# Loading q and k of tiles 2 to 5 of the first batch by token pairs, with VectorE and TensorE putting them in order, in a fused attention and MLP kernel with a hand-written order

## The chip, the cores and the metric

The kernel runs on one core of a Trainium2 chip. The metric is the device time of one execution in microseconds, the median of several runs. The clock that TensorE was granted stands at 1.000 in the profile shown.

## The reference, cut to what matters

Local attention with a few global keys, for 4 batches of 8 heads, 768 tokens and head dimension 64; its output, seen as 3072 tokens by 512, goes through an MLP of width 2048 with a squared ReLU.

```
scores = q @ k.T / sqrt(D)                      # (4, 8, 768, 768)
keep   = (key < 8) | (0 <= query - key < 96)    # 8 global keys, 96 local ones
scores = where(keep, scores - slope[h] * dist, -1e9)
attn   = softmax(scores) @ v                    # (4, 8, 768, 64)
x      = attn.transpose(0, 2, 1, 3).reshape(3072, 512)
out    = relu(x @ w_in) ** 2 @ w_out            # w_in 512x2048, w_out 2048x512
```

Since a query sees the keys of its own and of the preceding tile of 128 tokens, and the global ones, the kernel computes two 128x128 blocks of scores for each tile and head, "own" and "before".

## The kernel before

**Tiling.** A batch of 768 tokens is two halves of 384, and a half is three tiles of 128 tokens; the halves are H0 to H7. For each half come, in this order: loads of q, k and v from HBM with a cast from fp32 to fp16 (`list_loads`, `rows`, L491, issued by GpSimd, the engine POOL in the profile); q and k turned so that the head dimension lies on the partitions; scores (TensorE), exponentials (ScalarE, ACT in the profile), a product with a mask (VectorE, DVE), the product with v (`av`), a division (`norm`), the turn of the result into `xt`; then layer 1 (`hps`) and layer 2 (`yps`) of the MLP with fp16 weights, in part by a scheme that saves products by adding and subtracting blocks first (`in_mix`, `x_mix`, `mixed`, `w_mix`).

**The first batch, H0 and H1.** It is worked tile by tile, in the order that the list `OPENING` names: `T0`, `T1` turn tiles 0 and 1 (their q and k come by four HWDGE loads of token pairs in fp32, L539, which VectorE casts, L355), `Q2` to `Q5` and `K2` to `K5` turn the q and k of one tile (`turn_tile`, L1368: four 128x128 transposes into one PSUM bank, then one copy of 128x512), `P` puts the distance biases into PSUM (L1390), `S` adds the scores (L1411), `A` is the product with v (L1461), `X` turns its result (L1490), `F`, `G`, `D` and `E` are layer 1. q and k of tiles 2 to 5 come by eight loads of one tile each: 128 partitions, 8 heads, rows of 64 fp32 elements, 256 bytes each. Those of tile 2 land in `sk` and `sq`; those of tiles 3 to 5 land in the memory of `w_mix`, which nothing else uses so early. `LOADING` gives the order in which the loads of the first batch are numbered, with the four parts of `w_in` (c0 to c3) among them.

**The later halves.** H2 is turned by TensorE (`turn`, L650), H3 to H7 by DMA transposes on SP's queue (`turn_by_dma`, L670). `sk` and `sq` are single buffers: the loads of a half wait until the half before it has been turned. The results of attention go into `xt` by DMA transposes, too (`to_x_by_dma`, L801). The rows of the global keys of H3 are copied into `vb` by a DMA (`fix_globals`, L625).

**What sets the order.** Each step is an `Op` with its needs. The string `ORDER` lists all steps: `p` for TensorE's, by number, with the PSUM banks behind the point, `l` for the loads, and `a`, `d` and `s` for those of ACT, DVE and SP. `by_table` emits them in that order, so each engine's queue is fixed, in order, and an instruction that waits holds up everything behind it. A number behind `@` makes a load wait for a DMA transpose (six loads before, four in the changed kernel). The loads of POOL take turns on eight semaphores, so a load is issued only when the one eight places ahead of it has landed.

Of the kernel before, what the change touches and what calls it, by code (L numbers as in the profile page):

```python
# [10 lines left out]
FP16 = mybir.dt.float16  # L11
# [3 lines left out]
P = 128  # L15
# [5 lines left out]
OPENING = """T0 P1b T1 K3 P0o S0o S1b Q2 K2 P1o S1o P2o P2b A00 S2o A01 S2b Q5 Q3 A11 X01 Q4 V1 S3o A10  # L21
K4 X11 A20 X00 K5 X10 A21 S4o S4b S3b X21 X20 F1 G11 V2 S5o V3 S5b G10 F0 A40 V4 A30 G01 A41
# [4 lines left out]
LOADING = """v1 k3 k2 q2 v0 q3 q4 q5 k5 v2 k4 c1 v3 c0 v4 v5 c3 c2"""  # L27
# [26 lines left out]
ORDER = """d1 s8 g2 a4 p0.0 a6 s10 d12 a0 d13 l1 l2 l3 d146 a26 d15 d20 d3 a22 l0 a30 d9 d21 a18 d5 a17 a16  # L54
l4 d14 a19 p1.12 a27 p5.34 a28 d11 l5 a29 p10.56 d7 a23 l7 p3 l8 p4.7 l9 l6 a32 a31 a24 d37 p6 d33
a34 p2.07 a39 d35 p8.1 d36 p7 a40 d43 p11 l10 a25 a41 p9.2 p13.31 a46 d44 p12.40 l11 a42 d45 p14.2
d59 p17 a47 l12 p15 d48 a52 p16.5 p24.7 p19.6 d51 p20.2 a49 l13 d55 a53 p21.3 p18.5 d64 l14 a50
p28.4 p23.61 d56 a69 p27.7 d54 l16 p31.0 a57 d38 p26.4 p34.23 a60 d72 l17 p29.5 d68 p22.6 a61
p35.0 d70 l15 l18 a81 d58 p25.1 p30.7 a85 p36.2 d65 a82 p39.50 l23 d86 a71 d66 p32.63 a92 p33.12
d67 d63 l19 p40.74 a77 d91 p38.5 a78 d83 d62 d80 p37.1 a73 d79 d84 a74 p44.2 l22 p41.6 a93 d107  # L60
a87 d76 l21 p47.3 l20 a97 p52.2 p45.0 a89 d111 l27 d96 a119 p48.1 a98 d75 l28 a101 p46.3 l29 p43.7
d110 p53.5 p42.2 d105 l30 d95 p50.4 p55.6 a103 l25 p49.3 d116 d94 a120 a112 p59.7 l24 a102 d88
d106 a90 p51.4 a108 d189 p60.2 a114 d100 a104 d99 p56.5 a113 d191 a122 p57.1 p65.0 d125 p54.3 d138
a117 p63.6 p62.4 a128 d121 a109 p58.7 d139 d129 d130 p61.1 a118 p67.0 d115 a132 d272 d133 a131
p70.3 a135 p71.2 a126 d142 p72.1 p69.6 a162 d127 p82.4 d190 a156 d192 a165 p66.7 a159 l31 a157
a160 p64.0 d205 d158 l26 d163 a123 d161 p84.6 d134 a140 d206 l36 d143 d166 p83.3 d207 a136 l35
d164 p81.2 a167 d187 a141 p85 l33 d124 a137 d186 p79.57 a184 l34 l32 d147 p88.10 p80.34 a178 p77.2
a195 p74.5 a181 d201 d202 a196 d204 p68.1 d203 a179 d151 a182 p73.3 d208 d180 a144 p90.0 d183 a145
p86 a174 a168 d152 a169 p75.7 d154 p78.41 d153 p89.23 p87 a175 d148 a198 p100.5 a176 d155 a193
d150 p98.4 s194 l38 p91.2 a185 d197 l39 a199 d228 p76.1 a209 d177 a210 l37 p96.6 s229 a171 p105.3  # L70
p107 p92 d200 a172 d225 a173 p93.4 s216 p94 d170 a188 d149 p95.7 a211 a240 d236 s217 p97 d214 d219
d237 p104 d212 s220 p102.1 a245 p103.6 s226 d213 d238 a244 d227 d223 d221 p101 d218 p106 l45 a222
s224 p99 l41 d246 a241 s242 d239 s215 p109.47 d234 p108.06 p111 a251 a248 p118.2 d243 a252 d258
p110.14 l43 s235 s247 a249 d273 p116.07 l40 p113 d230 a255 l42 d250 l44@224 a256 d254 p112 a268
d253 d231 p119.6 d257 a269 p114.14 l47 d270 p115.07 p124 a261 d274 l46 p120 a283 d259 a264 s275
p122.1 a262 p129.6 d280 p121.5 s325 a265 d232 p127.0 d267 p126 d276 a287 p133.4 d285 p134.7 d295
a286 s324 p117.3 d263 a290 p123.4 a278 p140 d266 a271 p130 d281 a307 p128.5 p135 a291 a308 d233
p132 d298 p136 d294 a279 p131.3 d300 s282 a299 p137.1 l48@324 a297 p138 a303 d323 d301 p139 p125.4
a302 p142 d288 d304 a292 p143.7 d305 a310 d311 p141.1 d326 l49 s296 a284 a312 p144.6 a309 d293
s289 l52 a306 p145.53 d313 p146.02 p147.47 a327 d318 p148.1 a333 d433 d319 a322 l54 p149.5 a330  # L80
d336 a328 d314 l53 p151.41 d320 a331 p150.03 p152 a337 d329 l51 a338 d332 p157.2 a339 p153 d321
a341 d316 a344 a350 l50 a334 p172.0 l65 d315 a342 d345 p159.3 d340 p158.4 p161 d335 a355 p164.5
a352 p155.7 d370 p154.1 s277 p163 a347 d351 s371 p168.0 d395 p162 p169.4 d317 d358 a364 p156 a348
s398 p174.0 d356 a366 d343 a365 p171.7 d359 s399 l56 p177 p160.3 d369 a378 p165 l55 a360 p167 d357
s346 d353 a363 p173.5 p166.7 a372 p178.2 a362 s260 d373 p175 d349 a361 p180 d375 p182.3 s374 p179
d382 a379 p176 p170 d380 p183 d385 p181.0 a381 s354 p184 a376 a383 s386 p185.2 d367 d400 a387
p186.53 d384 a389 p188.71 a388 l60@371 p187.04 d368 d377 a413 l59 p189.6 a406 d401 d405 l57 a414
d402 p190.7 a409 d404 l62 d403 a407 p191 a410 l63 p193.51 a417 d416 a418 p194.03 d415 p192.46
l61@386 p195 d476 d411 a419 s390 d391 a426 l64 d408 l58 p196 p206.4 d393 a422 p198.0 d397 a420
p197.5 a434 d396 l74 a423 p219.6 d392 a432 d412 a427 d394 p210 d429 p218.1 a445 d477 a462 d424  # L90
p208 d480 a461 p204.7 d431 a448 p205.3 d421 p215.4 a444 p203.6 d443 p214 d442 a458 s491 l66 p199.1
# [209 lines left out]
def kernel(  # L301
# [1268 lines left out]
    jobs = {}  # L1570
# [115 lines left out]
```

## Time and profile before

| | us |
|---|---|
| three runs: median (lowest to highest) | 204.44 (203.87 to 205.93) |
| the profiled execution's own time | 204.62 |
| its span, first to last instruction | 202.8 |
| TensorE busy | 192.3 (95% of the span) |
| DVE busy | 177.4 (87%) |
| ACT busy | 146.5 (72%) |
| POOL busy | 66.7 (33%), nearly all of it issuing loads |

The profiled execution took 0.18 us more than the median of the runs; 1.8 us of its time lie outside its span. In the rows of the profile, PE is TensorE's matmul, PEld its weight load, and SPq and ACTq are the DMA issues of SP and ACT. A row of the timeline gives the start, the time until its last instruction ended, the engine, the line, what is written from what, and how many instructions were merged; in brackets stands the idle time ahead of it and what ended it.

### The profile page before, as it was taken

The page shows a single profiled execution, that of the slowest core. Times are in us where ns is not written, and L with a number is a line of the kernel's source. Part 1 is how long each engine was busy: PE and PEld are TensorE (multiplying, and loading weights), DVE is VectorE, ACT ScalarE, POOL GpSimd, SP SyncE. Part 2 cuts the span into 40 slices and gives each one's busy share as a digit, 9 for nine tenths or more (in the row PEclk, how much of TensorE's full clock was granted, in tenths as well). Part 3 has the DMA queues.
Part 4 walks back from the last instruction along what each step waited for, and adds up shares of the span by engine and source line. Part 5 has one row for each costly group of instructions (what it writes and reads, how often), then busy time and mean ns, then how long its engine had stood idle before and what let it go on. Part 6 is the DMA issues. An engine that isn't in the chain of part 4 may idle for free.

```text
span 202.8 us, 5878 instructions
## 1 busy us (share of the span) xinstructions
PE 192.3 (95%) x2348; PEld 161.7 (80%) x2348; DVE 177.4 (87%) x448; ACT 146.5 (72%) x310; POOL 66.7 (33%) x82
## 2 busy tenths in 40 slices
PE   7798999999999899999895999999999999999994
PEld 3676999866798587789783898889888899898993
DVE  6799789999995799999893999899999999989781
ACT  5799877988826679978783877977888676475221
POOL 8995637538006700790261702910000000000000
PEclk9999999999999999999999999999999999999999
DMA  5999999999999999999999993999632330020214
GB/s 158 177 148 193 198 178 176 206 187 157 167 182 114 192 132 166 91 177 131 221 128 140 96 180 81 164 165 147 179 109 73 95 80 15 0 107 0 103 55 155
DMA packets 106987, 27.52 MB, mean 136 GB/s; under 512 B 97104, under 2 KB 104016, under 8 KB 106960
## 3 DMA queue, kind: packets, MB, share of 16 engines
q0 software_dynamic: 74944, 13.11, 90.2%
q1 hardware_dynamic: 30816, 13.45, 31.6%
q10 hardware_dynamic: 1200, 0.59, 1.1%
q8 instruction: 18, 0.29, 0.7%
q14 instruction: 9, 0.07, 0.1%
HBM read 27.26 MB, written 6.29 MB: 165 GB/s over the span
## 4 chain that ended last, share of the span: by engine, by line
PE 44%; DMA 40%; POOL 8%; SPq 3%; issue 2%; DVE 2%; ACT 1%; POOLq 0%; DVEq 0%
PE yps L1145 22%; PE hps L925 14%; DMA sq<-in_q_dram 10%; DMA sk<-in_k_dram 7%; DMA w_out_sb<-in_moe_w_out_dram 6%; DMA xt<-tm 5%; PE hps L822 5%; DMA k<-sk 5%; DMA w_in_sb<-in_moe_w_in_dram 4%; POOL w_mix L491 3%; SPq L670 3%; DMA q<-sq 3%; POOL sk L491 2%; PE av L776 2%; POOL sq L491 2%
## 5 line engine op out<-in xcount | busy, mean ns | idle before, releaser
L822 PE MATMUL hps<-xt,w_in_sb 128*128 128x384 f16 (+2 forms) x336 | 45.4, 280 | 2.5 <-DMA xt<-tm 2.1
L728 ACT ACTIVATE ex<-sp 128x512 f16<-128x512 f32 x66 | 35.2, 619 | 7.1 <-PE sp L715 6.5
L1145 PEld LDWEIGHTS <-h 128*128 128x128 f16 x376 | 34.1, 98 | 4.5
L822 PEld LDWEIGHTS <-w_in_sb 128*128 128x128 f16 x336 | 28.1, 98 | 9.0 <-issue 0.9
L353 ACT COPY kept<-hps 128x384 f32<-128x384 f32 x43 | 20.2, 488 | 10.6 <-PE hps L925 8.5
L1145 PEld LDWEIGHTS <-mixed 128*128 128x128 f16 x272 | 25.3, 98 | 3.2
L491 POOL DMA_DIRECT2D sq<-in_q_dram x19 | 16.9, 895 | 33.2 <-DMA xt<-tm 16.4
L847 ACT ACTIVATE hr<-hps 128x384 f16<-128x384 f32 (+1 forms) x44 | 22.0, 546 | 6.7 <-PE hps L822 6.7
L491 POOL DMA_DIRECT2D v<-in_v_dram x24 | 21.6, 914 | 15.1 <-DMA k<-sk 12.8
L983 DVE CUSTOM_DVE_ANT_0 hr<-hps,kept 128x384 f16<-128x384 f32 x49 | 25.7, 548 | 0.8 <-PE hps L925 0.4
L353 ACT COPY y<-yps 128x256 f32<-128x256 f32 (+2 forms) x35 | 12.3, 381 | 18.2 <-PE yps L1145 17.0
L925 PEld LDWEIGHTS <-in_mix 128*128 128x128 f16 x272 | 22.9, 98 | 2.5 <-DVE x_mix L903 0.8
L925 PE MATMUL hps<-x_mix,in_mix 128*128 128x192 f16 x204 | 23.5, 246 | 0.4 <-ACT kept L353 0.4
L1145 PE MATMUL yps<-w_mix,h 128*128 128x256 f16 (+1 forms) x192 | 22.6, 264 | 0.0
L1145 PE MATMUL yps<-w_out_sb,h 128*128 128x256 f16 (+1 forms) x184 | 22.5, 268 | 0.0
L1145 PE MATMUL yps<-w_mix,mixed 128*128 128x256 f16 (+1 forms) x184 | 22.4, 268 | 0.0
L491 POOL DMA_DIRECT2D sk<-in_k_dram x19 | 16.9, 894 | 14.1 <-DMA k<-sk 9.0
L752 DVE TENSOR_TENSOR phat<-ex,mask 128x1024 f16<-128x1024 f16 (+1 forms) x36 | 20.6, 593 | 0.0
L925 PEld LDWEIGHTS <-w_in_sb 128*128 128x128 f16 x204 | 17.4, 98 | 3.1 <-issue 1.6
L1005 ACT ACTIVATE h<-hr 128x768 f16<-128x768 f16 x22 | 18.5, 850 | 1.5 <-DVE hr L983 0.9
L861 ACT ACTIVATE h<-hr 128x768 f16<-128x768 f16 (+1 forms) x23 | 16.8, 759 | 1.0 <-DVE hr L849 0.9
L925 PE MATMUL hps<-xt,w_in_sb 128*128 128x192 f16 x136 | 15.8, 246 | 0.0
(109 smaller groups left out, 350.6 us busy)
## 6 DMA issues: line engine op xcount, KB each, us to landing
out_dram<-y SPq DMA_DIRECT2D x23, 256.0 KB, 2.6
v<-in_v_dram POOLq DMA_DIRECT2D x24, 128.0 KB, 7.1
sk<-in_k_dram POOLq DMA_DIRECT2D x19, 128.0 KB, 6.6
sq<-in_q_dram POOLq DMA_DIRECT2D x19, 128.0 KB, 7.0
w_in_sb<-in_moe_w_in_dram POOLq DMA_DIRECT2D x4, 512.0 KB, 11.0
w_out_sb<-in_moe_w_out_dram POOLq DMA_DIRECT2D x4, 512.0 KB, 10.6
y<-in_q_dram SPq DMA_DIRECT2D x2, 256.0 KB, 4.3
y<-in_k_dram ACTq DMA_DIRECT2D x2, 256.0 KB, 5.0
```

What stands on the lines that cost most here:

```text
L353: nc.scalar.copy(out=out, in_=in_)
L491: dma = nc.gpsimd.dma_start(out=dst, in_=src[x.b, :, r0 + t * P:r0 + (t + 1) * P, :] .rearrange("h p d -> p h d"))
L670: turn = nc.sync.dma_start_transpose(out=turned_to(x, 1 - i).rearrange("p t a c -> p (t a) c"), in_=getattr(x, name).rearrange("p t h d -> ...
L728: nc.scalar.activation(out=st["ex"][:, h], in_=sp[h], func=AF.Exp, scale=scale)
L752: eng(e).tensor_tensor(out=x.phat[a][:, :, t0:t0 + n], op=ALU.mult, in0=st["ex"][:, :, i0:i0 + 2 * n].rearrange("p e (t b) c -> p e t (b c ...
L822: nc.tensor.matmul(st["ps"][:, i * n:(i + 1) * n], lhsT=w_in_sb[:, kk, m * P:(m + 1) * P], rhs=x.xt[:, kk, c0:c1], start=kk == 0, stop=kk ...
L847: nc.scalar.activation(out=o, in_=i, func=AF.Relu)
L861: nc.scalar.activation(out=h2, in_=hr, func=AF.Square)
L925: nc.tensor.matmul(st[name][:, i * HC:(i + 1) * HC], lhsT=left(i, kk), rhs=right(kk), start=fresh and i == kk == 0, stop=kk == KK - 1, ski ...
L983: nc.vector._custom_dve(TENSOR_ADD_SAT, out=hidden(which)[:, :, cols], in0=sums(name), in1=st[kept], s0=LARGEST, s1=0.0)
L1005: nc.scalar.activation(out=h2, in_=hr, func=AF.Square)
L1145: nc.tensor.matmul(st[bank_name][:, 0:n], lhsT=a(m), rhs=b(m)[:, cols], start=fresh and m == 0, stop=m == HK - 1, skip_group_check=not fresh)
```

## The change

- The eight loads of q and k of tiles 2 to 5 become four (`load_pair`): each brings two tiles of q or of k, partition p taking tokens 2p and 2p+1 of the 256, so that a contiguous piece is 512 bytes. All four land in the memory of `w_mix`.
- A new VectorE copy for each pair (`put_apart`, 128x1024 fp16, SBUF to SBUF) puts even and odd tokens apart.
- `turn_pair` takes the place of `turn_tile`: eight transposes for two tiles into one bank, and two copies of 128x512, one for each tile, that interleave even and odd tokens again. The number of transposes (32) and of these copies (8) stays.
- `OPENING` and `LOADING` lose the names that fell away, and `ORDER` is a new table over the whole kernel: the queues of all engines differ, from the first microseconds to the last store.

The core of the diff (`ORDER` by its last line; `rows_of_pair` and `paired`, which are added too, are called by nothing):

```diff
-LOADING = """v1 k3 k2 q2 v0 q3 q4 q5 k5 v2 k4 c1 v3 c0 v4 v5 c3 c2"""
+LOADING = """v1 k2 q2 v0 q4 v2 k4 c1 v3 c0 v4 v5 c3 c2"""
...
-s759 p363 p372 a750 p373 d762 s751 s763 a764 a765"""
+p359 a754 s755"""
...
+    def pair_of(i, r, apart=False):
+        if not pair_memory:
+            both = w_mix_memory()
+            pair_memory.append(both.rearrange("p i m d -> p (i m d)").rearrange(
+                "p (n c) -> p n c", n=8))
+        return pair_memory[0][:, (4 if apart else 0) + r - 2 + i]
+
+    def load_pair(i, r):
+        def emit(e):
+            return nc.gpsimd.dma_start(
+                out=pair_of(i, r).rearrange("p (h c) -> p h c", h=H),
+                in_=(k if i else q)[0, :, r * P:(r + 2) * P, :].rearrange(
+                    "h (p j) d -> p h (j d)", j=2))
+        pairs_in[i, r] = plan.load(plan.PAIRS, emit, [], None if plan.queues["LOAD"] else -3)
...
-    def turn_tile(r, i):
+    def turn_pair(r, i):
...
         def emit(e):
-            st["ps"] = ps = bank([P, NPAIR, P], FP16, "trp0")
+            st["ps"] = ps = bank([P, 2, NPAIR, P], FP16, "trp0")
...
             for a in range(NPAIR):
-                nc.tensor.transpose(out=ps[:, a], in_=(x.sk if i else x.sq)[:, t, 2 * a:2 * a + 2, :],
-                                    identity=ident)
-        job = plan.pe(0.29, emit, [(x.k_in if i else x.q_in)[t], ident_op], 1)
-        op = plan.after(job, {"ACT": 0.51, "DVE": 0.36}, lambda e: copy(
-            e, turned_to(x, i)[:, t], st["ps"]))
+                for j in range(2):
+                    nc.tensor.transpose(out=ps[:, j, a], in_=pair_of(i, r, True)[:, (j * NPAIR + a) * P:
+                                                                    (j * NPAIR + a + 1) * P],
+                                        identity=ident)
+
+        def put_apart(e):
+            copy(e, pair_of(i, r, True).rearrange("p (j h d) -> p j h d", j=2, h=H),
+                 pair_of(i, r).rearrange("p (h j d) -> p j h d", h=H, j=2))
+        apart = plan.add({"DVE": 0.33, "ACT": 0.96}, put_apart, [pairs_in[i, r]])
+        job = plan.pe(0.56, emit, [apart, ident_op], 1)
...
+        def evac(u):
+            x, t = halves[u // HT], u % HT
+            c = slice((u - r) * P // 2, (u - r + 1) * P // 2)
+            return plan.after(job, {"ACT": 0.51, "DVE": 0.6}, lambda e: copy(
+                e, turned_to(x, i)[:, t].rearrange("p a (c j) -> p a c j", j=2),
+                st["ps"][:, :, :, c].rearrange("p j a c -> p a c j")))
```

**The opening, ACT's queue.** Up to the first exponentials of the attention, `ph<-sp`, ACT's queue reads as follows before the change (`mask` and `slope_id` are tables made once, `trp` is the bank that holds transposes):

```order
L434 ACTIVATE mask<-dmask 128x384
L428 ACTIVATE slope_id<-ident 128x128
L434 ACTIVATE mask<-dmask 128x384
L428 ACTIVATE slope_id<-ident 128x128 x4
L434 ACTIVATE mask<-dmask 128x384 x4
L353 COPY k<-trp_175 128x512
L353 COPY q<-trp_162 128x512
L434 ACTIVATE mask<-dmask 128x384
L353 COPY k<-trp_175 128x512
L1431 ACTIVATE ph_89<-sp 128x512 x2
```

In the changed kernel the same stretch of ACT's queue, from behind the first five `slope_id`, is this:

```order
L435 ACTIVATE mask<-dmask 128x384 x3
L429 ACTIVATE slope_id<-ident 128x128 x2
L354 CAST sk<-y 128x2x256
L435 ACTIVATE mask<-dmask 128x384
L354 CAST sq<-y 128x2x256
L354 CAST sk<-y 128x2x256
L435 ACTIVATE mask<-dmask 128x384 x3
L354 COPY k<-trp_179 128x512
L354 COPY q<-trp_174 128x512 x2
L354 COPY k<-trp_210 128x512
L354 COPY k<-trp_179 128x512
L1469 ACTIVATE ph_89<-sp 128x512 x2
```

Three casts of the first tiles, two more copies out of PSUM and two more `slope_id` stand ahead of the first exponentials; before, VectorE did that work.

**The opening, POOL's queue.** Before the change the first loads are issued in this order, up to the first part of `w_in`:

```order
L491 DMA w_mix<-in_k_dram 128x8x64
L491 DMA sk<-in_k_dram 128x8x64
L491 DMA sq<-in_q_dram 128x8x64
L491 DMA v<-in_v_dram 128x8x64 x2
L491 DMA w_mix<-in_q_dram 128x8x64 x2
L491 DMA w_mix<-in_k_dram 128x8x64
L491 DMA v<-in_v_dram 128x8x64
L491 DMA w_mix<-in_q_dram 128x8x64
L491 DMA w_mix<-in_k_dram 128x8x64
L555 DMA w_in_sb<-in_moe_w_in_dram 128x4x512
```

In the changed kernel POOL's queue begins thus (a row of 128x8x128 is a pair):

```order
L487 DMA w_mix<-in_k_dram 128x8x128
L487 DMA w_mix<-in_q_dram 128x8x128
L516 DMA v<-in_v_dram 128x8x64
L487 DMA w_mix<-in_k_dram 128x8x128
L487 DMA w_mix<-in_q_dram 128x8x128
L516 DMA v<-in_v_dram 128x8x64 x2
L578 DMA w_in_sb<-in_moe_w_in_dram 128x4x512
```

Eleven issues stood ahead of `w_in`, now there are seven.

**The middle, SP's queue.** These are the transposes of H2's result into `xt` and of H3's q and k, and the copy of H3's global rows, `vb<-v`, before the change:

```order
L1075 DMA out_dram<-y 128x512
L801 DMA_TRANSPOSE xt<-tm 128x3x128
L670 DMA_TRANSPOSE k<-sk 128x12x128
L670 DMA_TRANSPOSE q<-sq 128x12x128
L801 DMA_TRANSPOSE xt<-tm 128x3x128 x3
L1230 DMA out_dram<-y 128x512
L625 DMA vb<-v 32x2x520
```

The same piece of SP's queue in the changed kernel:

```order
L1098 DMA out_dram<-y 128x512
L693 DMA_TRANSPOSE k<-sk 128x12x128
L693 DMA_TRANSPOSE q<-sq 128x12x128
L824 DMA_TRANSPOSE xt<-tm 128x3x128 x2
L648 DMA vb<-v 32x2x520
L824 DMA_TRANSPOSE xt<-tm 128x3x128 x2
L1253 DMA out_dram<-y 128x512
```

`vb<-v` has moved ahead of two transposes into `xt` and a store.

**The end, SP's queue.** The last stores before the change, where 128x128 is 64 KB and 128x512 is 256 KB:

```order
L1230 DMA out_dram<-y 128x512 x7
L1219 DMA out_dram<-y 128x256
L1230 DMA out_dram<-y 128x512
L1226 DMA out_dram<-y 128x128
L1681 UNCONDITIONAL_BRANCH
```

The last stores in the changed kernel:

```order
L1253 DMA out_dram<-y 128x512 x7
L1242 DMA out_dram<-y 128x256
L1249 DMA out_dram<-y 128x128
L1253 DMA out_dram<-y 128x512
L1719 UNCONDITIONAL_BRANCH
```

The last store is now one of 256 KB: the product that ends its tile (`p363` before, `p359` now) is TensorE's last, where it stood ahead of the two half-width products of the last tile.

More of the change, by code (lines that the diff above doesn't have):

```diff
@@ L59 @@
[L59 to L64, printed above, removed]
@@ L485, in list_loads, with rows_of_pair, emit @@
         vbefore = list(halves[x.hb - x.half - 3].attended) if x.hb >= 4 else []
+        def rows_of_pair(src, name, rank):
+            def emit(e):
+                return nc.gpsimd.dma_start(
+                    out=paired(x, name).rearrange("p h j d -> p h (j d)"),
+                    in_=src[x.b, :, r0:r0 + 2 * P, :].rearrange("h (p j) d -> p h (j d)", j=2))
+            return plan.load(plan.PAIRS, emit, before, rank)
         def rows(src, name, t, rank=None):
```

169 lines of the change are left out of this document (88 added, 81 removed).

## The prediction

> **What bounds the kernel now.** I read the busy time by stage first, then who TensorE waited for, then the chain of waits. The stretches, chosen at the places where TensorE idles:
>
> ```profile
> core 0: us, PE busy (x) PEld busy (x) DVE busy (x) ACT busy (x) POOL busy (x), PEclk, DMA share, GB/s
> 0.00:20.00 20.00, 16.46 (x246) 11.98 (x247) 16.43 (x54) 16.61 (x38) 17.24 (x25) 1.00 1.84 169
> 20.00:60.00 40.00, 39.96 (x479) 32.26 (x478) 37.10 (x96) 31.00 (x68) 17.95 (x21) 1.00 1.79 184
> 60.00:100.00 40.00, 39.11 (x480) 32.30 (x478) 34.42 (x84) 31.54 (x68) 15.74 (x18) 1.00 1.61 144
> 100.00:115.00 15.00, 11.99 (x142) 9.50 (x140) 11.84 (x31) 10.62 (x23) 8.57 (x10) 1.00 1.63 143
> 115.00:200.00 85.00, 84.79 (x1011) 75.69 (x1008) 77.61 (x187) 56.66 (x115) 7.20 (x9) 1.00 0.61 100
> ```
>
> The first number is the stretch, the second its length, the third TensorE's busy time. From 20 to 200 us TensorE is idle for 0.04 + 0.89 + 3.01 + 0.21 = 4.15 us only. So it is the bound there, and since the change leaves the number of matmuls as it is, it can gain only by an earlier start of that solid stretch, by less of the 4.15 us, or by a shorter end. The waits of TensorE name what is idle for:
>
> ```profile
> PE hps L822 <- DMA xt<-tm: 2.1, 2, 1.4
> PE av L776 <- DMA vb<-v: 0.9, 1, 0.9
> PE sp L715 <- DMA q<-sq: 0.5, 1, 0.5
> ```
>
> The columns are total us, times, longest. 3.5 us of the 4.15 are waits for DMAs. Why these are late stands in the chain of waits (start, length, what):
>
> ```profile
> 11.42 8.39 DMA w_in_sb<-in_moe_w_in_dram
> ...
> 32.56 12.67 DMA w_out_sb<-in_moe_w_out_dram
> ...
> 46.62 7.07 DMA sk<-in_k_dram
> ...
> 102.75 7.24 DMA xt<-tm
> ...
> 110.03 0.32 PE hps L822
> ```
>
> Up to 110 us the chain is one of loads: `w_in` waits behind the first token loads on POOL, `w_out` behind `w_in`, H3's last `sk` behind `w_out`, H3's transposes behind `sk`, H4's and H5's loads behind the transposes, and H4's `xt` transposes stand on SP behind H5's transposes. Whatever comes earlier at 11.42 can come earlier at 110.03.
>
> **The change, step by step.**
>
> *Loads (gain).* A single load takes POOL 0.89 us to issue, and the queue runs without a gap there:
>
> ```profile
> 1.37 1.04 POOL L491 DMA_DIRECT2D w_mix<-in_k_dram  x1
> 2.41 0.89 POOL L491 DMA_DIRECT2D sk<-in_k_dram  x1
> GB/s 158 177 148 193 198 178 176 206 187 157 167 182 114 192 132 166 91 177 131 221 128 140 96 180 81 164 165 147 179 109 73 95 80 15 0 107 0 103 55 155
> ```
>
> A pair has as many pieces as a single load (1024), so its issue costs 0.89 to 1.04 us (the two rows); I take 1.04. The first part of `w_in` is then issued at 1.37 + 4 x 1.04 + 3 x 0.89 = 8.2 us in place of 11.42: 3.2 us earlier. What the DMA engines need for a pair is in no row. Its lower end is one load, 0.89; its upper, two, 1.78. By bytes, 256 KB at the 206 GB/s of the best early slice are 1.27 us, which I take, since it lies between. Four pairs then save 4 x (1.78 - 1.27) = 2.0 us of transfer and 3.2 us of issue; the transfers decide once they queue, so the lead at `w_in` is 2.0 to 3.2 us, say 2.6. The Trainium skill, "DMA: Bandwidth & Descriptors", Specifications, gives 512 bytes as the least transfer for full rate; by its 435 GB/s a pair would be an estimated 0.6 us and the lead the upper 3.2. No row of before shows a 512-byte load on this queue.
>
> From there one load of v stands ahead of `w_out` that stood behind it: minus 0.89. So H3's last load leads by some 1.7 us. At H5, a load of v no longer stands ahead of its q and k, plus 0.89. H4's `xt` therefore leads by 2.6 us (bounds 2.0 to 3.2).
>
> *The middle (gain).* `vb<-v` of H3 moves ahead of two transposes on SP and away from H4's loads, so its 0.9 us go. What it passes was issued like this:
>
> ```profile
> 58.24 4.58 SPq L801 DMA_TRANSPOSE xt<-tm  x3
> ...
> 63.53 0.75 SPq L625 DMA_DIRECT2D vb<-v  x1
> ```
>
> Two transposes of H2 now come 0.75 us later for it, and TensorE waited for none of them before: nothing. With 0.9 us less waiting ahead of it, TensorE reaches H4's first scores and `xt` 0.9 us earlier, less what the opening loses (0.6, below), so the stalls of 0.5 and 2.1 us would become 2.9; the lead of 2.6 leaves 0.3. Against this stands a gate that fell away. Before the change POOL stopped H6's loads in the middle, until H4's last transpose had landed:
>
> ```profile
> 100.18 1.76 POOL L491 DMA_DIRECT2D sk<-in_k_dram  x2 [9.00 <-DMA k<-sk]
> ...
> 110.81 0.88 POOL L491 DMA_DIRECT2D sq<-in_q_dram  x1 [6.25 <-DMA xt<-tm]
> ```
>
> Now all loads of H6 may run beside H4's transposes. The last of these already took 7.24 us beside the loads that were let through; I charge half a load more, 0.5 us (bounds 0 and 4 x 0.89 = 3.6). The middle: 3.5 - 0.3 - 0.5 = 2.7 us gained; ends 3.5 and -0.1.
>
> *The opening (loss).* ACT carries the opening:
>
> ```profile
> 3.44 0.52 ACT L434 ACTIVATE mask<-dmask 128x384 f16<-128x384 f32 x1 [0.28 <-DVE dmask L413]
> 3.88 0.29 ACT L428 ACTIVATE slope_id<-ident 128x128 f16<-128x128 f16 x1
> ...
> 4.49 0.89 ACT L428 ACTIVATE slope_id<-ident 128x128 f16<-128x128 f16 x4
> 5.29 1.75 ACT L434 ACTIVATE mask<-dmask 128x384 f16<-128x384 f32 x4
> 8.05 0.59 ACT L353 COPY k<-trp 128x512 f16<-128x512 f16 x1 [1.02 <-PE trp L1325]
> 8.53 0.59 ACT L353 COPY q<-trp 128x512 f16<-128x512 f16 x1
> ...
> 9.90 1.11 ACT L1431 ACTIVATE ph<-sp 128x512 f16<-128x512 f32 x2
> ```
>
> Ahead of the first `ph<-sp` come two copies more, 0.48 us each by their starts (8.05, 8.53), two `slope_id` at 0.20 ((0.89 - 0.29) / 3), and three casts, whose price on ACT no row shows: 0.48 like the copy to 0.56 like `ph<-sp` (two in 1.11); I take 0.5, nearer to the copy. That is 2.9 us; it fills the idle 1.02 and 0.28 us. So the exponentials begin 1.6 us later, at 11.5. Before the attention of tile 2 ACT also gets one copy of the q4 pair, 0.48: its products start some 2.0 us later than here:
>
> ```profile
> 15.24 0.61 PEld L1461 LDWEIGHTS <-ph 128*128 128x128 f16 x16
> 17.32 0.41 DVE L355 COPY k<-trp 128x512 f16<-128x512 f16 x1
> 18.68 0.28 DVE L355 COPY xt<-trx 128x256 f16<-128x256 f16 x1
> 19.85 1.94 PE L822 MATMUL hps<-xt,w_in_sb 128*128 128x256 f16 x24 [0.45 <-DMA w_in_sb<-in_moe_w_in_dram]
> ```
>
> Layer 1 needs `xt`, complete at 18.96 before; 2.0 us later is 21.0, against its start at 19.85: 1.1 us lost if nothing in between gets shorter. What gets shorter: three transposes of tiles 4 and 5 and their VectorE copies (three of 0.41) stood between those products and `xt`, and now stand ahead of them; layer 1 would then begin at 20.3 or so, and one score block (about 0.2 us) is moved behind it. I take a loss of 0.6, ends 0 and 2.0. `w_in`, waited for 0.45 us here, lands by 8.2 + 8.4 = 16.6 us and costs nothing. The four new copies are hidden if a pair's copy ends before TensorE wants it; bounds for one are
>
> ```profile
> L355 DVE COPY kb<-k 128x1152 f16<-128x1152 f16 x2 | 0.9, 456 | 0.6 <-DMA k<-sk 0.6
> L355 DVE CAST sq<-y 128x512 f16<-128x512 f32 x2 | 1.5, 762 | 0.7 <-DMA y<-in_q_dram 0.7
> L491 POOL DMA_DIRECT2D w_mix<-in_q_dram x3: 903/1019/1042, 5.9 to 9.7; - x3
> w_mix<-in_k_dram POOLq DMA_DIRECT2D x3, 128.0 KB, 6.5
> ```
>
> The first two give the mean ns of one behind the busy time, the third least, median and most ns of an issue, the fourth the median us from issue to landing. 0.46 us (more elements, the same kind of copy) and 0.76 (a cast while POOL issues loads). The first pair is issued at 1.37 and lands near 1.37 + 6.5 + (1.27 - 0.89) = 8.2 us, the second 1.3 later, so q's copy ends at 10.3 at the latest, while the scores of tile 1 that stand behind its transposes wait for ACT's copies until 11: hidden, by 0.7 us. If the loads are later than that, the cost is one for one.
>
> The Trainium skill, "SBUF — State Buffer", Who interferes with whom, speaks against these copies: a VectorE copy in a two-port mode locks GpSimd out until it ends, and GpSimd then writes no descriptors. By that rule each of the four would hold an issue of POOL for its length, worked out below as a rival.
>
> *The end (loss).* The last store is 256 KB in place of 64:
>
> ```profile
> 199.83 0.27 ACT L353 COPY y<-yps 128x128 f32<-128x128 f32 x1 [0.52 <-PE yps L1145]
> L353 ACT COPY y<-yps 128x256 f32<-128x256 f32 x30 | 10.9, 388 | 15.9 <-PE yps L1145 14.7 <-issue 1.2
> out_dram<-y SPq DMA_DIRECT2D x3, 256.0 KB, 2.1
> out_dram<-y ACTq DMA_DIRECT2D x1, 64.0 KB, 1.7
> ```
>
> That is 0.39 - 0.27 = 0.12 us of copy and 2.1 - 1.7 = 0.4 of landing. The two half-width products now stand right behind what VectorE must hand out for them, with nothing between: one such addition, some 0.3 us, less the other half's 0.44 that covers part: 0.1. Sum 0.6, ends 0.4 and 1.0.
>
> **The sum.** On the profiled execution: 204.62 + 0.6 - 2.7 + 0.6 = 203.1. The median of the runs is 0.18 lower: 202.9 us, 0.7% less than 204.44.
>
> **Rivals.**
>
> 1. *The gate's place is taken by contention.* H6's loads slow H4's transposes by the full bound of 3.6 us; then only the 0.9 of `vb<-v` and some of `q<-sq` are gained. For it: the transpose of 7.24 us beside loads. Against: the loads are through sooner, too. 204.6 + 0.6 - 0.9 + 0.6 = 204.9, or 204.7 on the median.
> 2. *ACT becomes the bound of the opening (the other side).* Place: the exponentials of tiles 0 to 5, all on ACT, behind the added 2.9 us. If they hold the PSUM banks that the scores of tiles 4 and 5 and layer 1 wait for, TensorE loses the 1.6 us, two copies of 0.48 and the six exponentials (0.56 each) that keep three such pairs of banks: 5.9 us. A TensorE so late waits for none of the DMAs, which gives back all 3.5: 204.44 + 5.9 - 3.5 + 0.6 = 207.4. The kernel is slower from 2.9 us of loss on (3.5 - 0.6). For it: ACT is busy 16.6 of the first 20 us. Against: layer 1 of H0 stands in between as filler.
> 3. *The change doesn't do what it says:* a pair takes 1.78 us, as two loads. No lead: 0.9 gained in the middle, 0.6 + 0.6 lost: 204.7.
> 4. *VectorE's copies lock POOL:* each of the four holds an issue for 0.46 to 0.76 us, 2.4 in all, so the lead of 2.6 shrinks to 0.2: middle 1.1, sum 204.44 + 1.2 - 1.1 = 204.5. For it: issues beside VectorE's casts took up to 1.04 in place of 0.89, which would be only 0.6 in all.
> 5. *All waits go and the opening loses nothing:* 204.44 - 4.1 - 0.5 (`w_in`) + 0.6 = 200.4.
>
> **How the numbers follow.** The forecast has a chance of 0.48, with a range of its own from 201.4 to 204.2; rival 1 0.17; rival 2 0.13; rival 3 0.07; rival 4 0.05; rival 5 0.10. The range from 200.6 to 206.2 cuts half of rivals 2 and 5 and the forecast's edges: about 2 in 10 outside. About 1% (2.0 us) is what a measurement can tell from no change. Faster than 202.4 are rival 5 and half of the forecast: 0.34. Slower than 206.5 is rival 2: 0.13. Within 1%: 0.53.
>
> **What the profile after would show.** The first `w_in` issued near 8.2 us, landed by 17.5; the first `ph<-sp` at 11.5; layer 1's first matmul at 20.0 to 21; no wait `av` on `vb<-v` and under 1 us on `xt<-tm`; H3's `k<-sk` issued at about 52; the last store landing 0.4 us later behind TensorE's last matmul. Wrong would be: a wait of TensorE on ACT's exponentials above 1 us before 25 us, `w_in` landing after 19, or a new wait on a DMA after 115 us, where H6 and H7 now follow another order that I priced at nothing, since TensorE waited for nothing there.

## The result, and the profile after

The changed kernel takes 206.78 us in the median of 20 runs (204.32 to 209.53), the kernel before 204.42 in 20 runs beside them (203.07 to 206.47). The ratio is 1.0115, with a 95% interval from 1.0085 to 1.0144: about 1.2% slower, where 0.7% faster was forecast. Ratios here and below leave disturbed runs of either kernel out, so they can differ a little from those of the medians. The profiled execution of the changed kernel took 207.21 us, its span 205.4.

The same stretches as before, for the changed kernel (length, TensorE's busy time, clock, share and GB/s of the DMAs):

```profile
core 0: us, PE busy (x), PEclk, DMA share, GB/s
0.00:20.00 20.00, 14.62 (x204) 1.00 1.45 182
20.00:60.00 40.00, 40.00 (x502) 1.00 1.77 179
60.00:100.00 40.00, 38.66 (x473) 1.00 1.29 123
100.00:115.00 15.00, 13.06 (x153) 1.00 1.64 161
115.00:200.00 85.00, 84.12 (x999) 1.00 0.71 101
```

In the opening TensorE was busy for 16.46 - 14.62 = 1.84 us less than before, and the first matmul of layer 1 came 1.59 us later (21.44 in place of 19.85). The second number is the surer one: the kernel with `vb<-v` put back (below) has the same opening and the same 21.44, and its profile shows 15.84 us busy there, because its matmuls before 8 us took longer (the first eight, which only warm TensorE up, 3.60 us in place of 3.23). From 20 to 200 us it was idle for 0 + 1.34 + 1.94 + 0.88 = 4.16 us, against 4.15: of the 2.7 us that the middle should gain, nothing arrived. The waits after 60 us have other names, though (total us, times, longest; those for `vb<-v` and for ScalarE's `y` come after 115 us):

```profile
PE sp L738 <- DMA q<-sq: 1.9, 1, 1.9
PE hps L948 <- DVE hr L1006: 1.1, 1, 1.1
PE av L799 <- DMA vb<-v: 0.4, 1, 0.4
PE sp L738 <- ACT y L354: 0.4, 1, 0.4
PE hps L948 <- DMA xt<-tm: 0.2, 1, 0.2
```

The 2.1 us of `xt<-tm` have shrunk to 0.2, as was forecast; but TensorE now has a wait of 1.1 us ahead of that place, so this alone does not show the lead of the loads. In their place stand 1.9 us for H5's q and 1.1 us for a VectorE result. POOL's timeline says why. Before the change the loads of H4 ran through:

```profile
62.60 0.87 POOL L491 DMA_DIRECT2D sq<-in_q_dram  x1 [11.93 <-DMA q<-sq]
63.46 0.88 POOL L491 DMA_DIRECT2D sk<-in_k_dram  x1
64.33 0.89 POOL L491 DMA_DIRECT2D sq<-in_q_dram  x1
```

After it they begin 3.2 us earlier, and then stand still behind the first two:

```profile
59.39 1.76 POOL L516 DMA_DIRECT2D sq<-in_q_dram  x2 [9.41 <-DMA q<-sq]
67.52 1.76 POOL L516 DMA_DIRECT2D sk<-in_k_dram  x2 [6.37 <-DMA xt<-tm]
...
81.64 0.88 POOL L516 DMA_DIRECT2D sk<-in_k_dram  x1 [8.87 <-DMA k<-sk]
89.52 2.62 POOL L516 DMA_DIRECT2D sq<-in_q_dram  x3 [7.00 <-DMA xt<-tm]
```

The brackets name a transpose into `xt` for which these loads need not wait by their data: they are the gates that the table writes behind an `@`. H4's third load is issued at 67.52 in place of 64.33. The chain of waits of the changed kernel carries it from there to both stalls:

```profile
61.23 5.66 DMA xt<-tm
...
67.52 0.86 POOL sk L516
...
71.84 7.88 DMA v<-in_v_dram
79.82 0.28 DVE vb L356
80.10 0.93 DVE hr L1006 x2
...
82.90 5.76 DMA xt<-tm
...
89.52 2.62 POOL sq L516 x3
...
100.07 3.97 DMA q<-sq
104.17 0.85 PE sp L738 x24
```

H4's last v lands at 79.7; VectorE's copy of it stands ahead of `hr` in VectorE's queue, and TensorE waits for `hr`. The rest is H5: its second load stands at a gate, too, which names the transpose of H3 issued at 82.90, so its loads follow later (89.52), and so do its transposes and scores.

The transpose that H4's gate names was not issued late. It was issued at 61.23, and H2's last one before the change at 61.60; but it took 5.66 us to land where that one took 2.40. Two loads of H4 had been issued ahead of it, at 59.39 and 60.25, where before the first came at 62.60, behind the transposes. So two early loads were under way beside the very transpose for which the third one waits. That this is why the transpose took longer is argued from these rows; no run separates it.

### The profile page after: what moved, and what is told of

Its sections match the earlier page's. It is cut to its first block, busy times and chain, and to the rows that moved or that the text cites. A ratio compares the mean times of both kernels' runs of the same rounds, so it can differ in the third digit from the quotient of the medians.

```text
span 205.4 us, 5862 instructions
## 1 busy us (share of the span) xinstructions
PE 192.4 (94%) x2344; PEld 161.3 (79%) x2344; DVE 176.9 (86%) x447; ACT 150.3 (73%) x315; POOL 63.1 (31%) x78
## 4 chain that ended last, share of the span: by engine, by line
PE 42%; DMA 22%; DVE 14%; ACT 9%; POOL 5%; issue 4%; SPq 1%; ACTq 1%; POOLq 0%; DVEq 0%
PE yps L1168 16%; PE hps L845 12%; DMA xt<-tm 8%; PE hps L948 6%; DMA v<-in_v_dram 4%; DMA sk<-in_k_dram 3%; POOL sk L516 3%; POOL sq L516 3%; DVE phat L775 2%; DMA sq<-in_q_dram 2%; DMA k<-sk 2%; DVE hr L1006 2%; DMA q<-sq 2%; ACT ph L1469 2%; DVE tm L809 2%
## 5 line engine op out<-in xcount | busy, mean ns | idle before, releaser
L845 PE MATMUL hps<-xt,w_in_sb 128*128 128x384 f16 (+2 forms) x336 | 44.9, 280 | 0.0
L516 POOL DMA_DIRECT2D sk<-in_k_dram x18 | 16.0, 894 | 39.2 <-DMA xt<-tm 11.9
L354 ACT COPY kept<-hps 128x384 f32<-128x384 f32 x44 | 21.0, 488 | 7.1 <-PE hps L948 6.8
L516 POOL DMA_DIRECT2D sq<-in_q_dram x18 | 16.0, 897 | 30.4 <-DMA q<-sq 18.3
L516 POOL DMA_DIRECT2D v<-in_v_dram x24 | 21.5, 917 | 3.4 <-DMA w_in_sb<-in_moe_w_in_dram 1.7
L1028 ACT ACTIVATE h<-hr 128x768 f16<-128x768 f16 x23 | 19.1, 846 | 0.8 <-DVE hr L1006 0.8
L884 ACT ACTIVATE h<-hr 128x768 f16<-128x768 f16 (+1 forms) x21 | 15.5, 771 | 1.0 <-DVE hr L872 0.9
```

The source lines that it names most:

```text
L354: nc.scalar.copy(out=out, in_=in_)
L516: dma = nc.gpsimd.dma_start(out=dst, in_=src[x.b, :, r0 + t * P:r0 + (t + 1) * P, :] .rearrange("h p d -> p h d"))
L845: nc.tensor.matmul(st["ps"][:, i * n:(i + 1) * n], lhsT=w_in_sb[:, kk, m * P:(m + 1) * P], rhs=x.xt[:, kk, c0:c1], start=kk == 0, stop=kk ...
L884: nc.scalar.activation(out=h2, in_=hr, func=AF.Square)
L1028: nc.scalar.activation(out=h2, in_=hr, func=AF.Square)
```

## The experiments

Each kernel was compared with before on the same chip, in five rounds. The first four ran on one chip; the two in which H4's or H5's gates are gone, the kernel before with gates and the one with the end's order of before on a second; the other four on a third. The medians of before were 205.47, 204.89 and 204.50 us there, so a difference of some tenths of a per cent between kernels of different chips is not sure.

**The loads of the change in the order of before.** Each pair is issued where the first of its two loads stood, the copy that puts apart stands where the first transposes stood.

```diff
-                dma = nc.gpsimd.dma_start(out=dst, in_=src[...])           # one tile, k and q of tiles 2 to 5
+                    if (i, r) not in pair_loaded:
+                        pair_loaded[i, r] = nc.gpsimd.dma_start(out=pair_of(i, r)..., in_=src[0, :, r * P:(r + 2) * P, :]...)
...
+                copy("DVE", pair_of(i, r0, True)..., pair_of(i, r0)...)     # in turn_tile, once for a pair
-                nc.tensor.transpose(out=ps[:, a], in_=(x.sk if i else x.sq)[:, t, 2 * a:2 * a + 2, :], identity=ident)
+                for j in range(2):
+                    nc.tensor.transpose(out=ps[:, a, j * 64:(j + 1) * 64], in_=pair_of(i, r0, True)[c, ...], identity=ident[c, c])
```

> The kernel before with the loads of the change and nothing else: its table of the order stays, the first load of a pair that comes brings both tiles, VectorE's copy that puts the parities apart stands where the pair's first transposes stand, and each tile is turned out of half the partitions (eight transposes of 64 rows for four of 128) and evacuated by the interleaving copy. Theory A (the loads gain, the order loses): the first w_in is issued near 8 us in place of 11.42, and the kernel is 0.5 to 2 us faster than before, 202.5 to 204. Rival B (the loads themselves lose, by late pairs, the copy and the interleaving evacuation of 0.68 us in place of 0.41): the attention of tiles 2 to 5 and layer 1 come 1 to 2 us later, 205 to 206.5.

Measured: 207.64 us, ratio 1.0140 (1.0084 to 1.0195). `w_in` was issued at 8.99 as theory A has it, yet the time lies even above B's 205 to 206.5. This kernel also turns the tiles by 64 transposes of 64 rows where before needed 32 of 128, which the change does not do. TensorE waited for the copies, four times, and the clock that it was granted fell in two slices of the opening:

```profile
PE trp L1391 <- DVE w_mix L355: 2.8, 4, 1.0
PEclk9957999999999999999999999999999999999999
```

Layer 1 began at 24.68 us in place of 19.85. How much of the loss is the waits, how much the added transposes and how much the clock can't be told from one profile. Put into the old order in this way, the pairs lose.

**The order of the change with single loads.** Two single loads in the place of a pair, side by side where the copy would have put them; no copy, and plain evacuations.

```diff
-            return nc.gpsimd.dma_start(out=pair_of(i, r)..., in_=(k if i else q)[0, :, r * P:(r + 2) * P, :]...)
+            for j in range(2):
+                dma = nc.gpsimd.dma_start(out=pair_of(i, r, True)[:, j * H * D:(j + 1) * H * D]..., in_=(k if i else q)[0, :, (r + j) * P:(r + j + 1) * P, :]...)
...
-            copy(e, pair_of(i, r, True)..., pair_of(i, r)...)
+            return None
...
-                e, turned_to(x, i)[:, t].rearrange("p a (c j) -> p a c j", j=2), st["ps"][:, :, :, c].rearrange("p j a c -> p a c j")))
+                e, turned_to(x, i)[:, t], st["ps"][:, u - r]))
```

> The changed kernel with single loads again: each pair is two loads of one tile that land side by side where VectorE's copy would have put them, the copy falls away, the transposes are the same and the evacuation is a plain copy; the table of the order stays the changed one. Theory A (the loads gain, the order loses): w_in is issued some 2 to 3 us later than in the changed kernel, and the time is 0.5 to 2 us longer, 207.3 to 209. Rival B (the loads themselves lose): tiles 4 and 5 come no later than with pairs, VectorE's evacuations take 0.41 us again, layer 1 starts earlier than at 21.5 us, and the time is 1 to 2 us shorter, 205 to 206.

Measured: 208.36 us, ratio 1.0198 (1.0147 to 1.0248), against 1.0115 (1.0085 to 1.0144) with pairs: theory A. The first `w_in` was issued at 11.43, 2.6 us later than with pairs. In this order the pairs gain about 0.8%, and not in the opening: layer 1 began at 21.45, where it begins with pairs (21.44).

**The gates taken away.** Three `@` fall out of the table; every queue keeps its order.

```diff
-l37@228 ... l38@224 ... l50@286
+l37 ... l38 ... l50
```

> The changed kernel without the three gates that hold loads of H4 and H5 until a transpose into xt of the half before has landed. Theory A (these gates carry the two waits of TensorE after 60 us, 1.15 us for hr and 1.94 us for q<-sq): the loads of H4 run through from 59 or 62 us, those of H5 from 82, the waits for hr and q<-sq fall under 0.5 us each, waits on xt<-tm come back with at most 1 us, and the kernel is 1.5 to 2.5 us faster than the changed one, 204.3 to 205.3. Rival B (the gates keep the loads off the transposes): the waits on xt<-tm come back with 2 us or more, and the time stays within 0.5 us of the changed kernel's, 206.3 to 207.3.

Measured: 202.54 us, ratio 0.9930 (0.9892 to 0.9968): faster than before, and 4.2 us below the changed kernel by the medians (3.8 by the ratios), more than theory A expected. Its loads of H4 run through, and TensorE's only wait of more than 0.2 us after 60 us is this:

```profile
59.51 1.76 POOL L516 DMA_DIRECT2D sq<-in_q_dram  x2 [9.51 <-DMA q<-sq]
61.24 1.78 POOL L516 DMA_DIRECT2D sk<-in_k_dram  x2
...
PE hps L948 <- DVE x_mix L926: 0.8, 1, 0.8
```

VectorE's `x_mix` stands behind a wait of 0.96 us for `xt<-tm` there: that is all of the contention (theory B) that came back, and it is within theory A's 1 us.

**The three casts back on VectorE.** The three tokens go to VectorE, ahead of the first two copies that put apart.

```diff
-d9 s10 d37 d46 a22 ... a5 ... a11 a7
+d9 s10 d5 d11 d7 d37 d46 a22 ...
```

> The changed kernel with the three casts of the first tiles that it gave to ScalarE back on VectorE, ahead of the copies that put the first pairs apart, where VectorE was idle for 3.0 us. Theory A (ScalarE's queue carries the opening): the first exponential begins 0.5 to 1.5 us earlier than at 11.5, layer 1 earlier than at 21.5 by as much, and the time falls by 0.5 to 1.5 us, 205.3 to 206.3. Rival B (the opening waits for the late pairs of tiles 4 and 5 and their two evacuations one behind the other): the first exponential comes earlier, layer 1's first matmul stays within 0.3 us of 21.5, and the time is the same.

Measured: 207.47 us, ratio 1.0143 (1.0094 to 1.0192): no gain. ScalarE's first copies came 1.25 us earlier (7.79 in place of 9.04), but the exponentials only 0.1:

```profile
10.43 1.07 ACT L354 COPY k<-trp 128x512 f16<-128x512 f16 x2 [1.07 <-DVE k L356]
11.38 2.09 ACT L1469 ACTIVATE ph<-sp 128x512 f16<-128x512 f32 x4
```

ScalarE's copy for tile 3 stands ahead of the exponentials, and waits for VectorE's copy of tile 2 out of the same bank. In the changed kernel ScalarE reaches that copy at 10.52 without a wait. So the casts and the pair hold the exponentials up until almost the same time, and taking the casts away alone gains 0.1. Layer 1 began at 21.95, in a run whose clock fell there, so theory B's second number (within 0.3 of 21.5) is not confirmed.

**Each gate by itself.** First without the two of H4's loads:

```diff
-l37@228 ... l38@224 ... l50@286
+l37 ... l38 ... l50@286
```

> The changed kernel without the two gates of H4's loads; the gate of H5's loads stays. Theory A (each gate costs through its own half: H4's makes its loads of v late and so hr, H5's makes q<-sq late): H4's loads run through from 59 to 62 us, the wait for hr falls under 0.5 us, H5's loads still stop until a transpose of H3 has landed near 88, the wait on q<-sq stays at 1.5 us or more, and the time is 1 to 2 us below the changed kernel's, 204.8 to 205.8. Rival B (H4's gate is the whole loss, H5's gate only inherits its lateness): the time is 202 to 203.5, as without all three gates.

Then without that of H5's loads:

```diff
-l37@228 ... l38@224 ... l50@286
+l37@228 ... l38@224 ... l50
```

> The changed kernel without the gate of H5's loads; the two of H4's loads stay. Theory A (each gate costs through its own half): the wait for hr near 80 us stays at 1 us or more, the wait on q<-sq near 102 falls under 1 us, and the time is 1.5 to 2.5 us below the changed kernel's, 204.3 to 205.3. Rival B (H4's gate is the whole loss): q<-sq is still waited for by 1.5 us or more, and the time stays at 206 to 207.

Measured: without H4's gates 202.84 us, ratio 0.9933 (0.9900 to 0.9966), the same as without all three; without H5's 208.52 us, ratio 1.0199 (1.0147 to 1.0251). Rival B is right that the loss goes with H4's gates alone; its wait for q and its time for the kernel without H5's gate (206 to 207) did not come. H5's gate still held POOL without H4's, and it cost nothing: this kernel has no wait of TensorE over 0.2 us after 60 us.

```profile
85.22 2.63 POOL L516 DMA_DIRECT2D sq<-in_q_dram  x3 [5.30 <-DMA xt<-tm]
```

With H4's gates kept and H5's gone, H5's loads ran beside H3's late transposes, and the wait for q went, but a longer one for `xt` came:

```profile
PE hps L845 <- DMA xt<-tm: 2.5, 1, 2.5
PE hps L948 <- DVE hr L1006: 1.7, 1, 1.7
```

**The gates put into the kernel before**, at the third load of H4 and the second of H5.

```diff
-l43 s235 ... l52 a306
+l43@224 s235 ... l52@282 a306
```

> The kernel before with the gates where the changed kernel has them: the third load of H4 waits for H2's last transpose into xt, and the second of H5 for the second one of H3. Nothing else is changed. Theory A (the place of the gates alone makes the loss): H4's loads stop for 2 to 4 us near 64 us and H5's for 3 to 5 near 84, the waits of TensorE on q<-sq and on what follows H4's loads grow, and the time is 1 to 4 us above before, 205.5 to 208.5. Rival B (the gates cost only in the changed order, where the transposes that they name land later): the time stays within 1 us of before.

Measured: 204.22 us, ratio 0.9990 (0.9952 to 1.0028): rival B. The third load was issued without a wait:

```profile
62.86 0.88 POOL L491 DMA_DIRECT2D sq<-in_q_dram  x1 [12.06 <-DMA q<-sq]
63.72 0.88 POOL L491 DMA_DIRECT2D sk<-in_k_dram  x1
64.59 0.89 POOL L491 DMA_DIRECT2D sq<-in_q_dram  x1
```

By then the transpose had landed (64.27). The gate costs where the loads come ahead of the transpose that it names, and the transpose then lands late: this is what the change brought together.

**The copy of the global rows back behind the transposes**, with the gates kept.

```diff
-s224 ... s219 s228 s230
+s224 ... s228 s230 s219
```

> The changed kernel with its gates, and with the copy of H3's global rows back behind all four transposes of H2's result, as before the change. The gate of H4's third load names one of the two transposes that the copy had passed. Theory A (passing them costs, through the gate): that transpose is issued at about 60 us in place of 61.2, H4's third load at 66 to 66.5 in place of 67.5, TensorE's wait for hr falls by about 1 us, a wait on vb<-v of up to 0.9 us comes back, and the time falls by 0.5 to 1.5 us, to 205.3 to 206.3. Rival B (the transpose is late for another reason, and the copy's place does not matter): the third load stays at 67 us or later and the time within 0.5 us of the changed kernel's.

Measured: 207.38 us, ratio 1.0111 (1.0066 to 1.0156): rival B. The third load stayed where it was:

```profile
67.80 1.76 POOL L516 DMA_DIRECT2D sk<-in_k_dram  x2 [6.49 <-DMA xt<-tm]
```

In its chain of waits the transpose that the gate names follows VectorE's last `tm` of H2 (60.08), is issued at 60.67 and lands at 67.17. It is issued 0.56 us earlier than in the changed kernel, and takes 6.50 us in place of 5.66, again behind two loads of H4 (59.52 and 60.41). So the copy's place does not matter here.

**Single loads without the gates**, the edits of the second and the third experiment together.

> The changed kernel without the three gates and with single loads (two for each pair, no copy that puts apart, plain evacuations): what the pairs are worth where no gate stands behind them. Theory A (the lead of the pairs counts): w_in is issued 2.5 us later than with pairs and H3's last sk by 0.7 us or more, waits of TensorE on DMAs between 60 and 115 us come to 0.5 to 1.5 us, and the time is 203 to 204. Rival B (without the gates no load ends late, the lead is spare): 202.2 to 202.9, as with pairs.

Measured: 203.94 us, ratio 1.0000 (0.9965 to 1.0036), against 0.9930 (0.9892 to 0.9968) with pairs: theory A by the time. The pairs are worth about 0.7% here too, some 1.4 us by the medians; but the two kernels ran on different chips and their intervals touch. The new order without pairs and gates is as fast as the old one. The waits that were expected with it are not in its profile, which has none on a DMA over 0.2 us after 60 us; but that profile is of the fastest of its runs (202.93), so where the 1.4 us go in a usual run stays open.

**Plain copies in place of the interleaving ones**, without the gates.

```diff
-                e, turned_to(x, i)[:, t].rearrange("p a (c j) -> p a c j", j=2), st["ps"][:, :, :, c].rearrange("p j a c -> p a c j")))
+                e, turned_to(x, i)[:, t].rearrange("p a (j c) -> p j a c", j=2), st["ps"][:, :, :, c]))
```

> The changed kernel without the three gates and with plain copies out of PSUM for the pairs of tiles 2 to 5 in place of the interleaving ones: the tokens of these tiles are left in the order of their parities, so that their attention is not the reference's. Theory A (the interleaving copies, 0.68 us on VectorE where a plain one of before took 0.41, carry part of the opening's loss): layer 1's first matmul at 20.8 to 21.2 in place of 21.5, and 0.3 to 0.7 us off the time, 201.9 to 202.3. Rival B (the opening is carried by ScalarE's exponentials and by the order): the first matmul stays at 21.4 to 21.6, 202.5.

Measured: 202.21 us, ratio 0.9895 (0.9857 to 0.9933), against 0.9930 with the interleaving; the intervals overlap, so the time alone decides nothing. VectorE's copies took 0.41 us, and layer 1 began 0.7 us earlier than without the gates alone (21.56):

```profile
20.85 2.81 PE L845 MATMUL hps<-xt,w_in_sb 128*128 128x256 f16 x32
```

**The end's order of before**, without the gates.

```diff
-p369 a768 a769 p368 d766 s767 p359 a754 s755
+p359 a754 s755 p369 a768 a769 p368 d766 s767
```

> The changed kernel without the three gates, and with the full-width product that ends the last tile but one ahead of the two half-width products again, so that the last store is one of 64 KB. Theory A (the change of the end costs the 0.4 to 0.6 us that the prediction charged): 0.3 to 0.7 us below the kernel without the gates, 201.8 to 202.3. Rival B (the end of the span is set by TensorE's last product alone, and the store's size is hidden): no difference, 202.5.

Measured: 201.87 us, ratio 0.9872 (0.9825 to 0.9920), against 202.54 and 0.9930: 0.67 us by the medians, theory A's size, though the intervals overlap. Against the kernel without H4's gates, which ran on the same chip, it is 0.97 us. It has the lowest time of all versions, below both kernels.

**The ones of v written earlier as well**, on top of that.

```diff
-d1 g2 d12 a4 ... d17 d3 d150
+d1 g2 d12 d3 a4 ... d17 d150
```

> The changed kernel without the three gates, with the end's order of before, and with the ones of v written by VectorE ahead of the distances, so that POOL's third issue does not wait 1.1 us for them. Theory A (that wait holds up the pairs of tiles 4 and 5): the first w_in is issued near 7.8 us in place of 8.8, the pairs of tiles 4 and 5 are put apart 1 us earlier than at 12.8 and 14.1, layer 1 starts 0.3 to 0.6 us earlier, and the time is 201.2 to 201.6. Rival B (the opening waits for ScalarE): 201.9, as without that move.

Measured: 202.66 us, ratio 0.9972 (0.9926 to 1.0018): no gain. Whether it loses against the version without that move, which ran on another chip, is not shown. The first `w_in` was issued at 8.03 in place of 8.84, the pairs of tiles 4 and 5 were put apart only 0.3 and 0.35 us earlier (12.49 and 13.77), and layer 1 began at 21.51: rival B.

## Why the prediction was wrong, step by step

**The gates: the step that failed.** Under the middle, the prediction looked at the gate that fell away (H6's loads) and charged 0.5 us for it. The four gates in the new table got no price, although the table puts one of them at the third load of H4, where before the gate stood at the sixth and POOL reached it at 66.92, after the transpose had landed (64.00). At its new place it takes the lead of the loads away and 3.2 us more (67.52 in place of 64.33 for the third load). Without H4's two gates the changed kernel runs at 0.9933 of before, close to the forecast (202.9 / 204.44 = 0.9925). That it is so close is in part luck: without the three gates layer 1 begins 1.7 us later than before (21.56), where the opening was to lose 0.6, and TensorE is idle from 20 to 115 us for 0.78 us in place of 3.94, 3.2 us gained where 2.7 were forecast. Rival 1 spoke of the gates too, but in the other sense: contention after a gate had gone. Of that contention the kernel without the three gates shows at most the 0.8 us of `x_mix`, the one without H4's gates alone nothing; only with H4's gates kept and H5's gone it came to 2.5 us.

**The loads.** Their lead at `w_in` was right by its number: the first part was issued 2.6 us earlier, at 8.84. But 2.6 was the middle between 2.0 of transfers and 3.2 of issues, and it came about in another way, by luck: the issues led by more, and the third of them waited 1.13 us for VectorE's ones in `v`, which the forecast of 8.2 left out. The part landed only 1.75 us earlier (18.05 in place of 19.80), below the lower bound.

```profile
4.42 0.96 POOL L516 DMA_DIRECT2D v<-in_v_dram  x1 [1.13 <-DVE v L530]
...
8.84 0.80 POOL L578 DMA_DIRECT2D w_in_sb<-in_moe_w_in_dram  x1
```

The issues of pairs took 1.04, 0.89, 0.88 and 0.89, and the second pair landed 1.4 us after the first (the copies start at 7.93 and 9.37, both behind a wait for the load; forecast 1.27). So a pair costs less than two loads, and rival 3, which had no lead at all, is out. By the Trainium skill's rate ("DMA: Bandwidth & Descriptors", Specifications) the estimate was 0.6 us; the trace does not agree. The 1.27 counts the 256 KB written in fp16, at 206 GB/s, which stand in a slice after 35 us; the best of the first 20 us, 193, gives 1.36. The fp32 rows read for them are 512 KB, and which of the two sides sets the 1.4 us no run shows. What went wrong is the lead that was to arrive at H3: 0.56 us (the last `sk` at 46.06 against 46.62) in place of 1.7. A wait was missing from the working: `sk` is a single buffer, and H3's first `sk` waits until TensorE has turned H2. TensorE reached layer 1 1.6 us late, and this load came 1.9 us later than before (37.19), not earlier:

```profile
39.09 0.88 POOL L516 DMA_DIRECT2D sk<-in_k_dram  x1 [4.58 <-PE trp L673]
```

**The rest of the middle.** The wait for H3's `vb<-v` went, as forecast, and passing two transposes cost nothing (the experiment). After 115 us the kernel lost 0.88 us where nothing was priced: 0.4 us is a wait for a `vb<-v`, the new wait on a DMA there that the prediction named as a sign of being wrong, and 0.4 a wait for ScalarE's `y`. Without the gates no wait over 0.2 us stands there.

**The opening.** The first exponential came at 11.48 (forecast 11.5). In part this is luck: the sum of 2.9 us of added work has the three casts in it, 1.5 us, and without them the exponentials began only 0.1 earlier, because the pair's copies hold them too. Layer 1 began at 21.44, outside the 20.0 to 21 that was forecast, 1.6 us later than before, so the loss is 1.6 to 1.84 us, not 0.6. Part of it is a price that stood in the trace of before and was not used: the interleaving copy on VectorE, shown there by the first tiles' `q<-trp`, 0.69 us, where the plain copy takes 0.42.

```profile
8.33 0.42 DVE L355 COPY k<-trp 128x512 f16<-128x512 f16 x1 [0.84 <-PE trp L1368]
9.15 0.69 DVE L355 COPY q<-trp 128x512 f16<-128x512 f16 x1 [0.40 <-ACT q L353]
```

Five of the eight copies run on VectorE in the changed kernel, 0.27 us longer each; plain ones brought layer 1 0.7 us forward. The Trainium skill, "VectorE: DVE Perf Modes", What auto-detection actually checks, has the rule: the faster mode for a copy out of PSUM needs 16-bit tensors with steps of one. The trace agrees: 0.68 us on VectorE with the interleaving, 0.41 without, for the same 128x512 elements. By the code, the interleaving copy takes its elements in turn from the even and the odd tokens, which lie 512 elements apart in the bank. The other part is that the two tiles of a pair share a bank, and their copies on two engines come one behind the other:

```profile
17.74 0.68 DVE L356 COPY k<-trp 128x512 f16<-128x512 f16 x1
...
18.46 0.59 ACT L354 COPY k<-trp 128x512 f16<-128x512 f16 x1 [1.46 <-DVE k L356]
...
19.09 0.66 PE L1449 MATMUL sp<-q,kb 64*128 64x128 f16 x8 [0.93 <-ACT k L354]
```

Before, each tile had a bank and a copy of its own. That this costs what is left of the loss is argued from these rows; no run separates it, and the new order of the opening is a rival. Rival 2 had a loss in the opening by ScalarE's added work; taking the casts that it named away gained nothing. Its time of 207.4 is the nearest of all to the measured one, but by luck: it had 5.9 us lost in the opening and no wait on a DMA left. The copies that put apart took 0.41 to 0.52 us, about the lower bound. POOL's issues beside the first two of them took 0.91 us (v, at 7.98) and 0.94 (v, at 9.59), in place of 0.88, so rival 4's lock of 0.46 to 0.76 for each, after the rule of the Trainium skill ("SBUF — State Buffer", Who interferes with whom), does not show. The sums of rivals 3 and 4 have a slip besides. By the forecast's own terms the two stalls of 2.6 us become 2.9 less the lead, and H6's loads cost 0.5; so the middle would gain 0.1 us in rival 3 and 0.3 in rival 4, not 0.9 and 1.1, and their times would be 205.5 and 205.3.

**The end.** Forecast 0.6, measured 0.4 in the trace (from the last copy's start to the span's end 205.4 - 202.02 = 3.4 us, before 202.8 - 199.83 = 3.0) and 0.7 to 1.0 by the experiment's medians: right, as far as these can tell.

**The sum with what was measured:** 204.62 + 1.84 (opening) + 0.0 (middle) + 0.4 (end) = 206.9, against 207.21 in the profiled execution. With 1.59 for the opening it is 206.6.

## What to carry to other kernels

When a table of order or of gates is replaced, list every gate in it with the queue's place where it stands and the time at which its event lands, those that cost nothing before included: a gate that was free can bind when the loads behind it move earlier, all the more where they then run beside the very transfer that the gate names. A lead of loads is worth only what the next wait on another engine leaves of it, so a loss in the opening must be carried through single buffers into the loads. And where a copy changes its pattern, look for a row of the same pattern, not of the same size.

## What the runs showed of the hardware

The granted clock fell in the profiles of four kernels. In that of the old order it fell to 0.5 and 0.7 of full speed in two slices between 10 and 21 us, in a stretch with waits for VectorE's copies. In those without H4's gates and with the end's order it fell to 0.6 and to 0.8 and 0.5, in slices between 15 and 26 us, and in the run with the casts twice:

```profile
15.00:20.00 5.00, 3.55 (x67) 1.00 1.45 198
20.00:22.00 2.00, 2.00 (x30) 0.50 1.73 184
...
103.00:106.00 3.00, 1.28 (x27) 0.89 0.83 200
106.00:110.00 4.00, 4.00 (x26) 0.66 1.47 81
```

Both times a stretch in which TensorE was busy for less than its length (the clock is the number behind the count in brackets) went before, and the loss came after it, on full work. But such a stretch does not always bring it. The opening of the changed kernel and that without H4's gates are the same, and TensorE was busy for 1.63 and 1.01 us of the two pieces 16 to 18 and 18 to 20 us in the first, for 1.53 and 1.01 in the second; yet the clock stayed full in the one (the upper line) and fell in the other:

```profile
PEclk9999999999999999999999999999999999999999
PEclk9999699999999999999999999999999999999999
```

The Trainium skill, "TensorE: Matmul & The Clock Gate", What's actually happening, has half clock after an idle window of about 3.4 us. The half clock agrees; no idle time as long as that is in these rows, and no run here shows what set the clock.
